# Pack attention and two MLPs on one core: the first MLP's output projection in thirds over two batches, the packs' products moved between its row tiles

## The chip, the cores and the metric

The kernel runs on 1 core of one Trainium2 chip. The metric is the device time of one execution in microseconds (us). The kernel before takes 1770.42 us, the median of 3 runs (1769.96 to 1776.33).

## What is computed

The reference has three stages in float32. Eight batches of 576 tokens and 8 heads go through a two-step attention over 32 pack tokens a head; its output, 4608 tokens of 512 features, goes through a gated MLP and then through a second MLP:

```python
p_packed = sm_attn(p, k, v)
out = sm_attn(q, p_packed, p_packed)
...
xn = x / rms * rms_g
g = xn @ w_gate
silu = g * (1.0 / (1.0 + np.exp(-g)))
val = xn @ w_val
return (silu * val @ w_out)
...
h = x @ w_in
g = h * (1.0 / (1.0 + np.exp(-1.702 * h)))
return (g @ w_out)
```

d_model is 512, d_ff is 1536 in the first MLP and 2048 in the second.

## The kernel before, in words

Every product of two float32 matrices is made of three matmuls, since each operand is split into a high and a low part (`h` and `l` in the tiles' names): high by high, high by low, low by high.

**Units, steps, pairs.** The first MLP takes the batches two at a time: a unit u holds batches 2u and 2u+1, called o = 0 and o = 1 in the code, so there are 4 units. A unit has 12 steps, one for each 128 of the 1536 features, and two steps (G = 2) make a pair. There are 48 steps and 24 pairs.

**A step** has two parts. `prods(s)` (L606) multiplies the packs (tiles Lh, Ll) with this step's gate and value weights: 12 matmuls of 256 columns into two PSUM tiles `ps_w` (L624), each copied out by two ACT casts (Wh, L626) and two DVE subtractions (Wl, L627). `gateval(s, o)` (L642) multiplies Wh, Wl with a batch's attention weights, in halves of 288 tokens: four groups of 6 matmuls into `ps_g` (L655). Of each half ACT takes a tanh (L662) and DVE two products (L663, L665); then ACT casts the 576 tokens to Hh (L670) and GpSimd subtracts for Hl (L671).

**The projection.** After two steps `close` (L713) runs `project` (L675) for o = 0, then o = 1, and in each for the 4 row tiles m of the output, in halves of 288 tokens: 16 groups of 6 matmuls of 288 columns into `ps_o` (L686), 96 in a pair. In a unit's first pair ACT copies a group to the accumulator (L693). Later m = 1, and m = 3 outside unit 0, are added by DVE from PSUM (L696); the others are copied by ACT (L700) and both halves added by one GpSimd instruction (L702). At a unit's end the accumulators go to DRAM (L706).

**Around it.** `ps_w`, `ps_g` and `ps_o` share 5 PSUM banks. The products of step s+1 run inside the o = 0 gate of step s: half of them after its first group, half after its last (L726 to L732). The weights `wg` (3 buffers) and `wo` (2 buffers) are loaded through SP's queue (L599, L604) in units 1 to 3; in unit 0 they are converted piece by piece on ACT, DVE and GpSimd (L98). Every generator yields a number of nanoseconds, and the loop at L985 spends them: attention work of the next unit runs in between in units 0 to 2. In unit 3 there is none left; there `early` (L822) converts weights of the second MLP, one weight for every 9 yields.

The kernel's text isn't the order on the engines: the framework plans each engine's order ahead of time (`schedule_with_timeline_sim=True`, L1058), with the order in the text as priority, and an instruction whose operands the plan sees ready may pass an earlier one whose operands it doesn't. On the chip each engine then keeps that order and waits where an operand comes later than planned.

The second MLP (L850, L869) has 3456 matmuls of 512 columns and isn't touched.

Of the kernel before, what the change touches and what calls it, by code (L numbers as in the profile page):

```python
# [9 lines left out]
F32 = mybir.dt.float32  # L10
F32R = mybir.dt.float32r
# [17 lines left out]
def tile_pack_attention__then__two_mlps(  # L29
# [14 lines left out]
    nc = tc.nc  # L44
    B, H, S, D = q.shape
# [7 lines left out]
    NT = B * S  # L53
    P = 128
    HS = S // 2
    NC = -(-S // P)
    REST = S - (NC - 1) * P
    GROUPS = (range(NC // 2), range(NC // 2, NC))
# [8 lines left out]
    G = 2  # L67
# [457 lines left out]
    def mlp1(cv, lp, mm, getL, getAT):  # L525
# [116 lines left out]
        def gateval(s, o):  # L642
            u, j = steps[s]
            Wh, Wl = Wp[s]
            Ah, Al = Aq[u, o]
            th = main.tile([P, S], F32, tag="th", name="th", bufs=3)
            for e in range(2):
                cols = slice(e * HS, (e + 1) * HS)
                pst = []
                for c in range(2):  # L650
                    ps = mm.tile([P, 512], F32, tag="mm", name="ps_g")[:, :HS]
                    n = 0
                    for g in range(NG):
# [12 lines left out]
                    if (e, c) != (1, 1):  # L666
                        yield 730
            Hh = main.tile([P, S], F32R, tag="Hh", name="Hh", bufs=2 * G)
            Hl = main.tile([P, S], F32R, tag="Hl", name="Hl", bufs=2 * G)
            nc.scalar.copy(Hh, th)  # L670
            nc.gpsimd.tensor_sub(Hl, th, fl(Hh))  # L671
            hh[s, o] = Hh, Hl
            yield 730

        def project(ss, o, m):  # L675
            u, j0 = steps[ss[0]]
            b = 2 * u + o
            for e in range(2):
                cols = slice(e * HS, (e + 1) * HS)
                ps = mm.tile([P, 512], F32, tag="mm", name="ps_o")[:, :HS]  # L680
                n = 0
                for s in ss:
                    oh, ol = wo[s][:, 0], wo[s][:, 1]
                    Hh, Hl = hh[s, o]
                    for st, mv in ((oh, Hh), (oh, Hl), (ol, Hh)):
                        nc.tensor.matmul(  # L686
                            ps, st[:, m * P : (m + 1) * P], mv[:, cols], start=n == 0, stop=n == 3 * len(ss) - 1
                        )
                        n += 1
                if j0 == 0:  # L690
                    if e == 0:
                        acc[o, m] = main.tile([P, S], F32, tag=f"acc{o}{m}", name=f"acc{o}{m}", bufs=1)
                    nc.scalar.copy(acc[o, m][:, cols], ps)  # L693
                elif m == 1 or m % 2 and u:
                    a = acc[o, m][:, cols]
                    nc.vector.tensor_add(a, a, ps)  # L696
                else:
                    if e == 0:
                        t = main.tile([P, S], F32, tag="add", name="add", bufs=2)
                    nc.scalar.copy(t[:, cols], ps)  # L700
                    if e == 1:
                        nc.gpsimd.tensor_add(acc[o, m], acc[o, m], t)  # L702
                if e == 0:
                    yield 365 * G
            if j0 + len(ss) == NF1:
                nc.sync.dma_start(x2_d[b][:, m], acc[o, m])  # L706
            yield 365 * G

        def run():
            nonlocal main  # L710
            main = pools["main"]

            def close(ss):  # L713
                for s in ss:
                    have(wo, s)
                for o in range(2):
                    for m in range(NM):
                        yield from project(ss, o, m)
                for t in ss:
                    Wp.pop(t)  # L720
                    wo.pop(t)
                    used["wo"] = t + 1
                    for o in range(2):
                        hh.pop((t, o))
# [12 lines left out]
            yield from both(0, 0, prods(1))  # L737
            yield from both(1, 0)
            yield "attention"
            scaled(0, 1)  # L740
            yield "next"
            yield from both(0, 1)
            yield from both(1, 1, prods(2))
            yield from close([0, 1])
            for s, (u, j) in enumerate(steps):
                if s < G:
                    continue
                load_wo(s)
# [12 lines left out]
        return fetch, piece, run  # L761
# [2 lines left out]
    def mlp2(pre, banks):  # L764
# [57 lines left out]
        def early():  # L822
            load_w(0)
            load_w(1)
            for _ in range(10):
                yield
            for n in range(4):
                split_w(n, keep(n, pre))
                for _ in range(9):
                    yield  # L830
            for f in range(2, 2 + NEARLY):
                t = pre.tile([P, NM, TT], F32R, tag=f"x{'hl'[f % 2]}", name="w2_stage", bufs=1)
                t = t.rearrange("p (i x) f -> p i x f", i=2)
                for x in range(2):
                    split_w(2 * f + x, t[:, x])
                    for _ in range(9):
                        yield
                nc.sync.dma_start(w2_d[f], fl(t))
                yield
# [76 lines left out]
    with ExitStack():  # L916
# [8 lines left out]
        with ExitStack() as st1:  # L925
# [59 lines left out]
            for what in run():  # L985
# [18 lines left out]
                else:  # L1004
# [7 lines left out]
                    while done >= PIECE:  # L1012
                        done -= PIECE
                        piece()
        with ExitStack() as st3:
            pools["pa"] = st3.enter_context(tc.tile_pool(name="pa", bufs=1, space=PSUM))
            pools["pm"] = st3.enter_context(tc.tile_pool(name="pm", bufs=4, space=PSUM))
# [45 lines left out]
```

## Time and profile before

| what | value |
|---|---|
| median of 3 runs | 1770.42 us |
| the profiled execution | 1774.51 us |
| its span, first to last instruction | 1772.7 us |
| mean granted TensorE clock, as a share of full speed | 0.99 |
| PE busy | 1713.1 us (97%) |
| PE's share of the chain that ended last | 80% |

The first units lie at about 80 to 340 us (unit 0), 340 to 567 (unit 1), 567 to 784 (unit 2) and 784 to 971 (unit 3); the second MLP follows. A matmul's duration in the trace includes the time in which its columns pass through the array while the next one has begun, so busy sums are larger than the time taken: the start-to-start distance is what one matmul takes from the engine.

### The profile page before, as it was taken

The numbers are of one execution on the slowest core, as the hardware profiler recorded it, in microseconds if no ns is written. First come the engines' busy times: TensorE is split into PE (matmuls) and PEld (weight loads), VectorE is DVE, ScalarE is ACT, GpSimd is POOL, SyncE is SP. The second block draws the span as 40 slices with busy tenths as digits, with TensorE's granted clock in tenths as the row PEclk, the third lists the DMA queues.
The fourth block names the chain that finished last, engine by engine and source line by source line (L and its number), as shares of the span: only waits on it lengthen the run. The fifth ranks groups of instructions, "written<-read, shape, count | busy, mean of one in ns | idle before, by whom it ended". The sixth has DMA issues, their size and how long they took to land.

```text
span 1772.7 us, 26286 instructions
## 1 busy us (share of the span) xinstructions
PE 1713.1 (97%) x9976; PEld 1513.4 (85%) x9976; DVE 912.2 (51%) x1971; ACT 699.5 (39%) x1644; POOL 495.8 (28%) x470
## 2 busy tenths in 40 slices
PE   7899989999999999999998999999999999999998
PEld 4579889999999999999988788888888888888887
DVE  5688898746756566667875662222222222222221
ACT  4567666655545655556553321111111111111111
POOL 2355666734553455434453220000000000000000
PEclk9899999999999999999999999999999999999999
DMA  9655565543334432255644620000000000000000
GB/s 228 163 161 148 184 190 191 179 154 121 126 115 164 138 122 85 96 196 201 236 170 161 249 84 24 25 24 24 24 25 24 24 24 24 24 1 24 2 23 24
DMA packets 154463, 186.27 MB, mean 105 GB/s; under 512 B 87648, under 2 KB 124512, under 8 KB 147296
## 3 DMA queue, kind: packets, MB, share of 16 engines
q1 hardware_dynamic: 154336, 184.58, 32.3%
q8 instruction: 79, 1.29, 0.3%
q14 instruction: 48, 0.39, 0.1%
HBM read 139.46 MB, written 45.09 MB: 104 GB/s over the span
## 4 chain that ended last, share of the span: by engine, by line
PE 80%; DVE 9%; DMA 5%; ACT 3%; issue 2%; SPq 1%; POOL 0%; DVEq 0%; ACTq 0%; POOLq 0%
PE ps_dn L876 22%; PE ps_up L857 22%; PE ps_o L686 14%; PE ps_g L655 11%; PE ps_at L266 2%; PE ps_w L624 2%; DVE Wl L627 2%; PE ps_at L311 2%; PE ps_at L388 2%; PE ps_at L255 1%; DMA raw<-in_moe_w_in_dram 1%; DVE th L663 1%; DMA raw<-in_moe_w_gate_dram 1%; DVE between L110 1%; DMA raw<-in_moe_w_val_dram 1%
## 5 line engine op out<-in xcount | busy, mean ns | idle before, releaser
L857 PE MATMUL ps_up<-xh,wi 128*128 128x512 f32 x1152 | 381.6, 393 | 2.3 <-DMA wi<-w 1.7
L876 PE MATMUL ps_dn<-wo,gh 128*128 128x512 f32 x1152 | 356.7, 391 | 0.0
L686 PE MATMUL ps_o<-Hh,wo 128*128 128x288 f32 x1536 | 330.9, 301 | 14.9 <-ACT add L700 4.9
L860 ACT ACTIVATE gf<-ps_up 128x512 f32<-128x512 f32 x144 | 85.9, 597 | 611.0 <-PE ps_up L857 590.2
L863 DVE CAST gh<-gf 128x512 fp32r<-128x512 f32 x144 | 62.3, 433 | 508.1 <-ACT gf L860 508.0
L686 PEld LDWEIGHTS ps_o<-Hh,wo 128*128 128x128 f32 x1536 | 254.6, 190 | 21.2 <-ACT add L700 6.2
L857 PEld LDWEIGHTS ps_up<-xh,wi 128*128 128x128 f32 x1152 | 216.2, 188 | 52.1 <-POOL wo L113 2.0
L876 PEld LDWEIGHTS ps_dn<-wo,gh 128*128 128x128 f32 x1152 | 216.2, 188 | 47.5
L655 PE MATMUL ps_g<-Aqh,Wh 128*128 128x288 f32 x768 | 235.6, 307 | 9.0 <-DVE th L663 4.4
L686 PE MATMUL ps_o<-Hl,wo 128*128 128x288 f32 x768 | 228.0, 298 | 0.0
L655 PE MATMUL ps_g<-Aqh,Wl 128*128 128x288 f32 x768 | 227.2, 297 | 0.0
L655 PE MATMUL ps_g<-Aql,Wh 128*128 128x288 f32 x768 | 226.7, 295 | 0.0
L857 PE MATMUL ps_up<-xl,wi 128*128 128x512 f32 x576 | 225.8, 392 | 0.0
L876 PE MATMUL ps_dn<-wo,gl 128*128 128x512 f32 x576 | 224.6, 391 | 0.0
L671 POOL TENSOR_TENSOR Hl<-th,Hh 128x576 fp32r<-128x576 f32 x96 | 137.6, 1433 | 207.6 <-ACT Hh L670 183.4
L655 PEld LDWEIGHTS ps_g<-Aqh,Wh 128*128 128x128 f32 x768 | 144.9, 189 | 16.6 <-DVE th L663 6.8
L702 POOL TENSOR_TENSOR acc<-acc,add 128x576 f32<-128x576 f32 x90 | 129.9, 1444 | 69.1 <-ACT add L700 68.5
L686 PEld LDWEIGHTS ps_o<-Hl,wo 128*128 128x128 f32 x768 | 146.1, 190 | 0.1
L655 PEld LDWEIGHTS ps_g<-Aqh,Wl 128*128 128x128 f32 x768 | 144.6, 188 | 1.0 <-DVE Wl L627 0.7
L655 PEld LDWEIGHTS ps_g<-Aql,Wh 128*128 128x128 f32 x768 | 145.0, 189 | 0.0
L627 DVE TENSOR_TENSOR Wl<-ps_w,Wh 64x512 fp32r<-64x512 f32 x192 | 131.7, 686 | 25.6 <-ACT Wh L626 22.2
L626 ACT CAST Wh<-ps_w 64x512 fp32r<-64x512 f32 x192 | 111.4, 580 | 46.4 <-PE ps_w L624 30.3
(150 smaller groups left out, 2591.3 us busy)
## 6 DMA issues: line engine op xcount, KB each, us to landing
wg<-wg SPq DMA_DIRECT2D x48, 1024.0 KB, 5.0
wo<-wo SPq DMA_DIRECT2D x48, 512.0 KB, 4.1
x<-acc SPq DMA_DIRECT2D x32, 288.0 KB, 2.4
out_dram<-ob SPq DMA_DIRECT2D x36, 256.0 KB, 2.0
vn<-in_v_dram SPq DMA_DIRECT2D x16, 512.0 KB, 5.4
qn<-in_q_dram SPq DMA_DIRECT2D x64, 128.0 KB, 3.6
raw<-in_moe_w_in_dram SPq DMA_DIRECT2D x16, 512.0 KB, 3.8
raw<-in_moe_w_out_dram SPq DMA_DIRECT2D x16, 512.0 KB, 3.5
```

Source lines behind the costliest of these rows:

```text
L266: nc.tensor.matmul(ps, x[:, a], y[:, a, span(e)], start=n == 0, stop=n == len(todo) - 1)
L311: nc.tensor.matmul(o, x[: size(c), c], v_of(y, c), start=i == 0, stop=i == len(todo) - 1,)
L626: nc.scalar.copy(Wh[rows, :, g], src)
L627: nc.vector.tensor_sub(Wl[rows, :, g], src, fl(Wh[rows, :, g]))
L655: nc.tensor.matmul(ps, st[:, o, g, c * P : (c + 1) * P], mv[:, g, cols], start=n == 0, stop=n == 3 * NG - 1)
L671: nc.gpsimd.tensor_sub(Hl, th, fl(Hh))
L686: nc.tensor.matmul(ps, st[:, m * P : (m + 1) * P], mv[:, cols], start=n == 0, stop=n == 3 * len(ss) - 1)
L702: nc.gpsimd.tensor_add(acc[o, m], acc[o, m], t)
L857: nc.tensor.matmul(ps, st[:, i], mv[:, i], start=n == 0, stop=n == 3 * NM - 1)
L860: nc.scalar.activation(gf, ps, AF.Gelu_apprx_sigmoid)
L863: nc.vector.tensor_copy(gh, gf)
L876: nc.tensor.matmul(pacc[r], st[:, r * P : (r + 1) * P], mv, start=f == 0 and n == 0, stop=f == NF2 - 1 and n == 2,)
```

## The change

The two batches of a unit lie behind each other in one tile (Hh, Hl and the accumulators have 1152 columns in place of 576), and `project` goes through them in thirds of 384 tokens: 4 row tiles by 3 thirds, 12 groups of 6 matmuls, 72 in a pair. The second third holds tokens of both batches. A third is added by a GpSimd instruction of its own. The products of the next two steps stand between the row tiles of `close`: one of their four groups behind each. `load_wo` of both steps stands at the pair's start, and `load_wg` behind both gates of a step. The nanoseconds yielded change with it (3 by 486 for 2 by 365 a batch), and `early` waits 8 yields for 9.

```diff
+    TS = 2 * S // 3
...
-            Hh = main.tile([P, S], F32R, tag="Hh", name="Hh", bufs=2 * G)
-            Hl = main.tile([P, S], F32R, tag="Hl", name="Hl", bufs=2 * G)
+            if o == 0:
+                hh[s] = [main.tile([P, 2, S], F32R, tag=f"H{x}", name=f"H{x}", bufs=G) for x in "hl"]
+            Hh, Hl = (t[:, o] for t in hh[s])
             nc.scalar.copy(Hh, th)
             nc.gpsimd.tensor_sub(Hl, th, fl(Hh))
...
-        def project(ss, o, m):
+        def project(ss, m):
+
             u, j0 = steps[ss[0]]
-            b = 2 * u + o
-            for e in range(2):
-                cols = slice(e * HS, (e + 1) * HS)
-                ps = mm.tile([P, 512], F32, tag="mm", name="ps_o")[:, :HS]
+            for e in range(3):
+                cols = slice(e * TS, (e + 1) * TS)
+                ps = mm.tile([P, 512], F32, tag="mm", name="ps_o")[:, :TS]
...
-                    if e == 0:
-                        t = main.tile([P, S], F32, tag="add", name="add", bufs=2)
-                    nc.scalar.copy(t[:, cols], ps)
-                    if e == 1:
-                        nc.gpsimd.tensor_add(acc[o, m], acc[o, m], t)
-                if e == 0:
-                    yield 365 * G
+                    t = main.tile([P, TS], F32, tag="add", name="add", bufs=3)
+                    nc.scalar.copy(t, ps)
+                    a = acc[m][:, cols]
+                    nc.gpsimd.tensor_add(a, a, t)
+                if e < 2:
+                    yield 486 * G
             if j0 + len(ss) == NF1:
-                nc.sync.dma_start(x2_d[b][:, m], acc[o, m])
-            yield 365 * G
+                for o in range(2):
+                    nc.sync.dma_start(x2_d[2 * u + o][:, m], acc[m][:, o * S : (o + 1) * S])
+            yield 486 * G
...
-            def close(ss):
+            def close(ss, ahead=()):
...
-                for o in range(2):
-                    for m in range(NM):
-                        yield from project(ss, o, m)
+                rest = (ns for s in ahead for ns in prods(s))
+                for m in range(NM):
+                    yield from project(ss, m)
+                    yield next(rest, 0)
+                yield from rest
...
-            yield from both(1, 1, prods(2))
-            yield from close([0, 1])
-            for s, (u, j) in enumerate(steps):
-                if s < G:
-                    continue
-                load_wo(s)
-                yield from both(s, 0, prods(s + 1))
-                load_wg(s + WGB)
-                yield from both(s, 1)
-                if j == NF1 - 1:
+            yield from both(1, 1)
+            Wp.clear()
+            yield from close([0, 1], [2, 3])
+            for s in range(G, len(steps), G):
+                u, j = steps[s]
+                ss = list(range(s, s + G))
+                for t in ss:
+                    load_wo(t)
+                for t in ss:
+                    for o in range(2):
+                        yield from both(t, o)
+                    Wp.pop(t)
+                    load_wg(t + WGB)
+                last = j + G == NF1
+                if last:
                     yield "attention"
                     scaled(u + 1, 0)
                     scaled(u + 1, 1)
-                if j % G == G - 1:
-                    yield from close(list(range(s - G + 1, s + 1)))
-                if j == NF1 - 1:
+                yield from close(ss, [t + G for t in ss])
+                if last:
                     yield "unit"
...
-            for _ in range(10):
+            for _ in range(6):
                 yield
...
-                for _ in range(9):
+                for _ in range(8):
                     yield
```

## Rows read from the trace of the kernel before

**Rows 1.** The page: busy time of the engines, and the granted clock in slices.

```profile
PE 1713.1 (97%) x9976; PEld 1513.4 (85%) x9976; DVE 912.2 (51%) x1971; ACT 699.5 (39%) x1644; POOL 495.8 (28%) x470
...
PEclk9899999999999999999999999999999999999999
```

**Rows 2.** Busy time by stretch: unit 0, unit 3, second MLP (stretch, length, busy).

```profile
80.00:340.00 260.00, 240.66 (x1677) 222.32 (x1677) 223.22 (x576) 178.80 (x483) 159.09 (x168) 0.97 0.55 170
...
784.00:971.00 187.00, 176.60 (x1286) 170.81 (x1284) 139.86 (x265) 103.30 (x212) 86.65 (x63) 0.99 0.55 193
971.00:1772.70 801.70, 794.83 (x3456) 648.35 (x3456) 225.53 (x387) 129.27 (x221) 20.24 (x15) 1.00 0.11 38
```

**Rows 3.** The same view for most of units 1 and 2.

```profile
350.00:750.00 400.00, 400.00 (x3016) 390.71 (x3015) 246.03 (x550) 223.15 (x546) 182.56 (x162) 1.00 0.39 124
```

**Rows 4.** Waits of PE in unit 3: total us, times, longest us.

```profile
PE ps_g L655 <- DVE Wl L627: 3.3, 3, 2.6
PE ps_g L655 <- DVE th L663: 2.1, 3, 0.9
PE ps_w L624 <- DVE th L665: 1.0, 1, 1.0
```

**Rows 5.** Timeline of PE: a projection's first matmul, and the next pair's first gate matmul.

```profile
891.72 0.29 PE L686 MATMUL ps_o<-Hh,wo 128*128 128x288 f32 x1
...
904.47 0.29 PE L655 MATMUL ps_g<-Aqh,Wh 128*128 128x288 f32 x1
```

**Rows 6.** Groups by line and shape: instructions that are cut anew or moved.

```profile
L686 PE MATMUL ps_o<-Hh,wo 128*128 128x288 f32 x1536 | 330.9, 301 | 14.9 <-ACT add L700 4.9 <-DVE th L663 4.3 <-ACT acc L693 2.5
...
L671 POOL TENSOR_TENSOR Hl<-th,Hh 128x576 fp32r<-128x576 f32 x96 | 137.6, 1433 | 207.6 <-ACT Hh L670 183.4 <-issue 16.8 <-PE ps_w L624 3.1
L627 DVE TENSOR_TENSOR Wl<-ps_w,Wh 64x512 fp32r<-64x512 f32 x192 | 131.7, 686 | 25.6 <-ACT Wh L626 22.2
L702 POOL TENSOR_TENSOR acc<-acc,add 128x576 f32<-128x576 f32 x90 | 129.9, 1444 | 69.1 <-ACT add L700 68.5
L626 ACT CAST Wh<-ps_w 64x512 fp32r<-64x512 f32 x192 | 111.4, 580 | 46.4 <-PE ps_w L624 30.3 <-DVE Wl L627 13.7
...
L700 ACT COPY add<-ps_o 128x288 f32<-128x288 f32 x180 | 70.3, 400 | 95.4 <-PE ps_o L686 94.5
```

**Rows 7.** Timeline of PE in the second MLP: eight matmuls of 512 columns.

```profile
1299.62 0.39 PE L857 MATMUL ps_up<-xl,wi 128*128 128x512 f32 x1
...
1301.44 0.62 PE L876 MATMUL ps_dn<-wo,gh 128*128 128x512 f32 x2
```

**Rows 8.** Timeline of PE in unit 3: a wait, and 12 matmuls later.

```profile
947.55 0.58 PE L655 MATMUL ps_g<-Aqh,Wh 128*128 128x288 f32 x1 [2.61 <-DVE Wl L627]
...
950.57 0.31 PE L655 MATMUL ps_g<-Aqh,Wh 128*128 128x288 f32 x1
```

**Rows 9.** Sums over unit 3's six gate stretches (first group to projection).

```profile
sum 106.29, PE 98.42 PEld 94.12 DVE 90.94 ACT 67.12 POOL 39.90; mean PE 16.40 PEld 15.69 DVE 15.16 ACT 11.19 POOL 6.65
```

**Rows 10.** Sums over unit 3's six projections.

```profile
sum 80.68, PE 78.15 PEld 76.66 DVE 48.92 ACT 36.17 POOL 46.72; mean PE 13.03 PEld 12.78 DVE 8.15 ACT 6.03 POOL 7.79
```

**Rows 11.** Timelines of PE, DVE, ACT and POOL: last gate group to Hl, unit 3.

```profile
859.58 0.29 PE L655 MATMUL ps_g<-Aqh,Wl 128*128 128x288 f32 x1
...
862.25 0.45 DVE L665 SCALAR_TENSOR_TENSOR th<-th,ps_g 128x288 f32<-128x288 f32 x1
...
862.73 0.68 ACT L670 CAST Hh<-th 128x576 fp32r<-128x576 f32 x1 [0.83 <-DVE th L665]
...
861.98 1.44 POOL L702 TENSOR_TENSOR acc<-acc,add 128x576 f32<-128x576 f32 x1 [2.38 <-ACT add L700]
863.49 1.43 POOL L671 TENSOR_TENSOR Hl<-th,Hh 128x576 fp32r<-128x576 f32 x1
```

**Rows 12.** The page, DMA issues: KB each, median us to landing.

```profile
wg<-wg SPq DMA_DIRECT2D x48, 1024.0 KB, 5.0
wo<-wo SPq DMA_DIRECT2D x48, 512.0 KB, 4.1
```

More of the change, by code (lines that the diff above doesn't have):

```diff
@@ L667, in gateval @@
                         yield 730
-            Hh = main.tile([P, S], F32R, tag="Hh", name="Hh", bufs=2 * G)
-            Hl = main.tile([P, S], F32R, tag="Hl", name="Hl", bufs=2 * G)
+            if o == 0:
+                hh[s] = [main.tile([P, 2, S], F32R, tag=f"H{x}", name=f"H{x}", bufs=G) for x in "hl"]
+            Hh, Hl = (t[:, o] for t in hh[s])
             nc.scalar.copy(Hh, th)
             nc.gpsimd.tensor_sub(Hl, th, fl(Hh))
-            hh[s, o] = Hh, Hl
             yield 730
-        def project(ss, o, m):
+        def project(ss, m):
             u, j0 = steps[ss[0]]
-            b = 2 * u + o
-            for e in range(2):
-                cols = slice(e * HS, (e + 1) * HS)
-                ps = mm.tile([P, 512], F32, tag="mm", name="ps_o")[:, :HS]
+            for e in range(3):
+                cols = slice(e * TS, (e + 1) * TS)
+                ps = mm.tile([P, 512], F32, tag="mm", name="ps_o")[:, :TS]
                 n = 0
@@ L683, in project @@
                     oh, ol = wo[s][:, 0], wo[s][:, 1]
-                    Hh, Hl = hh[s, o]
+                    Hh, Hl = (t.rearrange("p o t -> p (o t)") for t in hh[s])
                     for st, mv in ((oh, Hh), (oh, Hl), (ol, Hh)):
@@ L691, in project @@
                     if e == 0:
-                        acc[o, m] = main.tile([P, S], F32, tag=f"acc{o}{m}", name=f"acc{o}{m}", bufs=1)
-                    nc.scalar.copy(acc[o, m][:, cols], ps)
+                        acc[m] = main.tile([P, 2 * S], F32, tag=f"acc{m}", name=f"acc{m}", bufs=1)
+                    nc.scalar.copy(acc[m][:, cols], ps)
                 elif m == 1 or m % 2 and u:
-                    a = acc[o, m][:, cols]
+                    a = acc[m][:, cols]
                     nc.vector.tensor_add(a, a, ps)
                 else:
-                    if e == 0:
-                        t = main.tile([P, S], F32, tag="add", name="add", bufs=2)
-                    nc.scalar.copy(t[:, cols], ps)
-                    if e == 1:
-                        nc.gpsimd.tensor_add(acc[o, m], acc[o, m], t)
-                if e == 0:
-                    yield 365 * G
+                    t = main.tile([P, TS], F32, tag="add", name="add", bufs=3)
+                    nc.scalar.copy(t, ps)
+                    a = acc[m][:, cols]
+                    nc.gpsimd.tensor_add(a, a, t)
+                if e < 2:
+                    yield 486 * G
             if j0 + len(ss) == NF1:
-                nc.sync.dma_start(x2_d[b][:, m], acc[o, m])
-            yield 365 * G
+                for o in range(2):
+                    nc.sync.dma_start(x2_d[2 * u + o][:, m], acc[m][:, o * S : (o + 1) * S])
+            yield 486 * G
         def run():
@@ L711, in run @@
             main = pools["main"]
-            def close(ss):
+            def close(ss, ahead=()):
                 for s in ss:
                     have(wo, s)
-                for o in range(2):
-                    for m in range(NM):
-                        yield from project(ss, o, m)
+                rest = (ns for s in ahead for ns in prods(s))
[3 more added lines that the diff above has]
+                yield from rest
                 for t in ss:
-                    Wp.pop(t)
                     wo.pop(t)
+                    hh.pop(t)
                     used["wo"] = t + 1
-                    for o in range(2):
-                        hh.pop((t, o))
             def both(s, o, ahead=None):
@@ L835, in early @@
                     split_w(2 * f + x, t[:, x])
-                    for _ in range(9):
+                    for _ in range(8):
                         yield
@@ L1014, in tile_pack_attention__then__two_mlps @@
                         piece()
+            for _ in ahead:
+                pass
         with ExitStack() as st3:
```

## The prediction

> **What bounds the kernel now.** I read the page first: PE is busy for 97% of the span and the granted clock is near full in all slices [rows 1], so only fewer PE nanoseconds or fewer PE waits can change the time. Busy time by stretch then tells where PE idles. The second MLP, 801.7 us of the span, isn't touched. Over 400 us of units 1 and 2 PE has no idle time at all [rows 3]. Unit 0 leaves 260.0 - 240.7 = 19.3 us idle and unit 3 187.0 - 176.6 = 10.4 us [rows 2]. So the steady state is bound by the rate at which PE takes columns, and the two outer units lose some to waits. Third, the waits in unit 3: PE waits 3.3 us for Wl, the packs' products on their way out through DVE, and 2.1 and 1.0 us for the gate's products in `th` [rows 4]. Last, the timeline, for the distance from one matmul to the next: a projection's 96 matmuls take 904.47 - 891.72 = 12.75 us [rows 5], 132.8 ns each, while the mean duration on the page is 301 [rows 6].
>
> **Part A: 72 matmuls of 384 columns for 96 of 288.** The columns are the same, so what goes is whatever each matmul costs beside its columns. No row has 384 columns. The nearest are 288 at 132.8 ns and 512, eight of which take 301.44 - 299.62 = 1.82 us [rows 7], 227.5 ns each. The line through both gives 132.8 + 96 x 94.7/224 = 173.4 ns for 384. 72 x 173.4 = 12.48 us for 12.75: 0.27 us a pair, **6.4 us** over 24 pairs. The whole second MLP is slower, 801.7/3456 = 232.0 ns [rows 2]; the line to that gives 175.3 ns and 3.1 us saved, which is one bound. The other end is the rows' rounding: if the eight took 1.81 us, the line gives 172.8 ns and 7.4 us. I take 6.4, from matmuls in a row at full clock like the projection's.
> The fixed part can be held against a rule. The Trainium skill, "TensorE: Matmul & The Clock Gate", section "Back-to-back issue gap", gives N/2.4 + 2.5 ns for the distance at full clock. By that 576 matmuls would save 1.4 us; here the trace disagrees with 132.8 ns, where the rule gives 122.5.
>
> **Part B: the products leave the gate.** In a pair 24 matmuls, 8 ACT casts of 580 ns and 8 DVE subtractions of 686 ns [rows 6] move from the gate into the projection. PE's own work is the same. What it frees is in unit 3, where weight conversions share DVE: there DVE is busy 90.9 of 106.3 us in the gate stretches [rows 9] and 48.9 of 80.7 in the projections [rows 10]. Taking 8 x 0.686 = 5.5 us a pair out leaves DVE (90.9 - 32.9)/6 = 9.7 us in a gate that takes 12.8 us of PE; the projection goes to (48.9 + 32.9)/6 = 13.6 us in about 15.3. Then: the waits for Wl go, 3.3 us, since each product now has at least two row tiles or a whole gate of the first step ahead of its use. With the 2.61 us wait goes what it did to the clock: the 12 matmuls behind it took 950.57 - 947.55 = 3.02 us [rows 8] where 12 x 0.1328 = 1.59, nearly twice as long each, as at the lower of the clock's two levels: 1.4 us. Of the 3.1 us for `th` I take half, 1.5 (bounds 0 and 3.1). What is late next is the projection itself, whose PSUM banks wait for DVE and ACT: 0.5 us back (bounds 0 and 3). **B = 5.7 us**, bounds 1.7 and 7.8. Outside unit 3 I take nothing from B: units 1 and 2 have no idle time to give.
>
> **Part C: the projection needs o = 1 sooner.** Before, a projection began with o = 0 and came to o = 1 after 48 matmuls, 6.4 us. Now its second third holds tokens of o = 1. In the text's order 6 matmuls of the first third, 3 of the first step and one with Hh come before the first that reads the late Hl: 10 x 0.173 = 1.7 us. In unit 3 Hl came later than that: the last gate matmul starts at 859.58, DVE ends `th` at 862.70, ACT Hh at 863.41, and GpSimd, which does an addition first, Hl at 864.92 [rows 11]: 5.2 us after the projection's first matmul at 859.71. So 3.5 us are uncovered if PE keeps the text's order. But the plan knows DVE, ACT and GpSimd's queues too (that the addition is ahead of Hl shows that it expected Hh no earlier), and it has work to pull forward: the first thirds of three more row tiles, 18 x 0.173 = 3.1 us, and the packs' products, 24 x 0.119 = 2.9 us by the line of part A at 256 columns. Cover is 6.0 us, if PSUM banks are free. What remains is the time by which the chip is later than the plan. In units 1 and 2, full of attention work tied together as closely, this leaves no idle time [rows 3]: 0 there. In units 0 and 3 ACT and DVE wait for converted weights, which the plan can't know; I take 0.35 us a pair for 12 pairs, **4 us** lost (bounds 0 and 24 x 3.5 = 84, if no work is pulled forward).
>
> **Part D: edits without a price.** ACT's copies and GpSimd's additions are cut anew: ACT 3 copies of 400 to 533 ns (as is, or by columns) for 4 of 400, GpSimd 3 additions of 963 to 1444 ns for 2 of 1444 [rows 6]. GpSimd may grow by 45 x 1.444 = 65 us at worst, but it is 28% busy [rows 1]; in unit 3's projections it is busy 7.8 of 13.4 us [rows 10], and if that cover is gone the additions delay Hl, which is part C. `load_wo` of both steps waits at the pair's start for the last projection's end; behind it on SP's queue stand weights for conversion and `wg`. The load lands in 4.1 us, `wg` in 5.0 [rows 12], and the projection is a gate of 12.8 us away, so nobody waits; `load_wg` no longer waits for products, which by then lie a projection back. The stores at a unit's end go out two by two, with the second MLP's reads much later. `early` has 8 of 192 yields a weight for 9 of 216: the same pace. Hh's buffer is freed at the projection's end for both batches; its next writer comes after four gate groups, 3.2 us. Unit 0 gets another order of conversions, with ACT's projection fuller: between 5 us better and 10 worse, taken as 0, since its total work is the same.
>
> **Sum.** -6.4 - 5.7 + 4 = -8.1 us. The profiled execution took 1774.51 us (span 1772.7 and 1.8 around it), so one like it would take 1766.4. The median of the runs is 4.1 us below that execution; I give the time on the median's scale: **1762.3**, or 1762.
>
> **Rivals.** *The columns cost what they cost* (0.15): spacing is proportional, 384 take 177.1 ns and A is nothing; 1768.7. For it: the second MLP's mean of 232.0 ns is near proportional (236.1). Against: eight of its matmuls in a row at 227.5. The rule of the Trainium skill named above would put it between, at 1767.3. *The projection waits for Hl* (0.14): slower. The place is the second third of the first row tile in each pair; price 3.5 us a pair if nothing is pulled forward, and with half of it covered 24 x 1.75 = 42 us, in place of the 4 taken: 1800. It decides from (8.85 + 12.1)/24 = 0.87 us a pair on. For it: Hl comes 5.2 us late in the row, with an addition ahead of it. Against: units 1 and 2 without idle time. *More waits go* (0.16): unit 0 also profits, 5 us of its 19.3, C costs nothing and `th` no longer waits: -6.4 - 7.3 - 5 = -18.7; 1752. The forecast itself has 0.55, between 1756 and 1768.
>
> **The numbers.** About 0.5% (8.85 us) is what a measurement of this kernel can tell from no change; the bounds are 1761.6 and 1779.3. The forecast lies next to the lower one: of its 0.55 I give 0.23 to faster and 0.32 to same; the third rival adds 0.16 to faster, the first 0.15 to same, and of the second 0.13 is slower and 0.01 same. Faster 0.39, same 0.48, slower 0.13. The range leaves out the dear end of the Hl wait and the best end of the third rival: 1750 to 1778.
>
> **What would show it.** A: L686's count is 1728 and a projection's 72 matmuls without a gap take 12.5 us plus the products' 2.8. B: no wait on Wl is left in unit 3, its gate stretches shrink from 17.7 us towards 13, DVE's busy time in them to about 10. C: PE's waits at L686 for Hl or Hh sum to some 4 us, all in units 0 and 3. I am wrong if units 1 and 2 show idle time at the second third, if unit 0 grows by over 10 us, or if 384 columns are spaced at 177 ns.

## The result, and the profile after

The changed kernel takes 1740.1 us, the median of 4 runs (1738.92 to 1741.57), against 1770.19 us before: a ratio of 0.9819, 95% interval 0.9803 to 0.9836. It is 30 us faster, where 8 were forecast, and below the range of the forecast. The profiled execution took 1741.26 us with a span of 1739.5.

The page of the changed kernel, busy times and clock, beside [rows 1]:

```profile
PE 1698.6 (98%) x9400; PEld 1501.6 (86%) x9400; DVE 908.5 (52%) x1936; ACT 690.1 (40%) x1583; POOL 502.3 (29%) x515
...
PEclk9899999999999999999999999999999999999999
```

To see where 33.3 us of span went (the profiled execution before lies 4.3 us above its median, the one after 1.2 us), I cut both traces at the first gate matmul of each unit and at the second MLP's first matmul. Busy time by stretch, the kernel before: units 0 to 3, second MLP (stretch, length, then busy time of PE and PEld, TensorE's matmuls and weight loads, DVE, which is VectorE, ACT, which is ScalarE, and POOL, which is GpSimd):

```profile
90.77:357.42 266.65, 248.60 (x1761) 232.59 (x1761) 223.48 (x575) 180.01 (x479) 169.92 (x175) 0.98 0.56 177
357.42:567.20 209.78, 209.78 (x1582) 204.84 (x1581) 129.17 (x287) 117.23 (x288) 94.69 (x83) 1.00 0.40 130
567.20:784.03 216.83, 213.99 (x1617) 209.23 (x1616) 137.55 (x302) 122.69 (x296) 96.92 (x87) 1.00 0.39 128
784.03:971.30 187.27, 176.57 (x1286) 170.81 (x1285) 140.01 (x265) 103.30 (x212) 86.67 (x63) 0.99 0.55 193
971.30:1772.74 801.44, 794.83 (x3456) 648.32 (x3456) 225.38 (x386) 129.27 (x221) 20.18 (x14) 1.00 0.11 38
```

The same stretches of the changed kernel:

```profile
88.16:341.61 253.45, 245.84 (x1652) 231.42 (x1652) 226.24 (x576) 183.16 (x478) 172.81 (x191) 0.99 0.60 187
341.61:551.43 209.82, 209.82 (x1441) 203.52 (x1439) 129.98 (x280) 113.88 (x267) 98.07 (x95) 1.00 0.42 132
551.43:760.69 209.26, 209.26 (x1450) 204.66 (x1448) 133.17 (x287) 116.78 (x274) 95.72 (x94) 1.00 0.38 128
760.69:938.50 177.81, 170.07 (x1130) 165.40 (x1129) 137.26 (x253) 99.33 (x196) 87.70 (x72) 1.00 0.58 205
938.50:1739.46 800.96, 794.85 (x3456) 648.38 (x3456) 225.49 (x386) 129.57 (x221) 20.50 (x14) 1.00 0.11 38
```

Unit 0 is 13.2 us shorter, units 1 and 2 together 7.5, unit 3 9.5, the second MLP 0.5. The stretch ahead of the first gate is 2.6 us shorter, but in the experiments' traces it lies between 84.0 and 91.0 us for kernels whose text is the changed kernel's up to there, so I count it for nothing.

Columns: a projection of unit 3 without a wait, in the timeline of PE:

```profile
833.41 0.33 PE L687 MATMUL ps_o<-Hh,wo 128*128 128x384 f32 x1
...
848.06 0.40 PE L625 MATMUL ps_w<-wg,Lh 128*128 128x256 f32 x2
...
848.77 0.29 PE L656 MATMUL ps_g<-Aqh,Wh 128*128 128x288 f32 x1
```

The last of four product groups takes 0.71 us; 15.36 - 4 x 0.71 = 12.52 us for 72 matmuls, 173.9 ns each. Before it was 12.75 for 96 [rows 5]: 0.23 a pair, 5.5 us over 24.

What the prediction never looked at is unit 0 by its stages. Sums over its six gate stretches and its six projections, the kernel before, then after:

```profile
sum 156.39, PE 145.92 PEld 135.06 DVE 147.80 ACT 112.54 POOL 83.89; mean PE 24.32 PEld 22.51 DVE 24.63 ACT 18.76 POOL 13.98
sum 110.26, PE 102.68 PEld 97.53 DVE 75.68 ACT 67.47 POOL 86.03; mean PE 17.11 PEld 16.26 DVE 12.61 ACT 11.25 POOL 14.34
```

```profile
sum 117.01, PE 115.02 PEld 109.02 DVE 114.14 ACT 82.41 POOL 65.83; mean PE 19.17 PEld 18.17 DVE 19.02 ACT 13.73 POOL 10.97
sum 136.44, PE 130.82 PEld 122.41 DVE 112.10 ACT 100.75 POOL 106.97; mean PE 21.80 PEld 20.40 DVE 18.68 ACT 16.79 POOL 17.83
```

Before, DVE was busy 147.80 of 156.39 us in unit 0's gates, 95%, and 69% in its projections. PE was idle for 156.39 - 145.92 = 10.5 us in the gates and 7.6 in the projections; after it is 2.0 and 5.6.

The granted clock has a part in it too. Three of unit 0's six projections before and one after hold a piece at 0.50, the lower of the clock's two levels (stretch, length, busy times, then the mean granted clock):

```profile
118.86:140.40 21.54, 19.01 (x127) 18.00 (x127) 13.66 (x34) 14.73 (x37) 12.65 (x16) 0.92 0.69 210
167.71:188.40 20.69, 18.68 (x127) 17.74 (x126) 16.96 (x46) 13.58 (x37) 17.98 (x20) 0.92 0.53 168
262.08:279.91 17.83, 16.30 (x109) 15.84 (x109) 13.15 (x36) 9.83 (x29) 14.10 (x14) 0.90 0.56 177
```

```profile
197.06:224.18 27.12, 24.97 (x149) 23.32 (x148) 24.26 (x64) 17.22 (x44) 22.07 (x28) 0.94 0.57 182
```

Each piece begins about where a wait of PE ends, of 1.2 to 2.5 us, for a copy by ACT. Length times what the clock lacks to 1.00 gives 5.2 us lost before and 1.6 after, so some 3.5 of unit 0's 13.2 us are clock that came back with the waits.

### The profile page after: what moved, and what is told of

Its sections match the earlier page's. It is cut to its first block, busy times and chain, and to the rows that moved or that the text cites. A ratio compares the mean times of both kernels' runs of the same rounds, so it can differ in the third digit from the quotient of the medians.

```text
span 1739.5 us, 25121 instructions
## 1 busy us (share of the span) xinstructions
PE 1698.6 (98%) x9400; PEld 1501.6 (86%) x9400; DVE 908.5 (52%) x1936; ACT 690.1 (40%) x1583; POOL 502.3 (29%) x515
## 4 chain that ended last, share of the span: by engine, by line
PE 86%; DVE 5%; DMA 4%; ACT 2%; issue 1%; POOL 1%; DVEq 0%; ACTq 0%; SPq 0%; POOLq 0%
PE ps_dn L882 23%; PE ps_up L863 23%; PE ps_o L687 14%; PE ps_g L656 14%; PE ps_w L625 3%; PE ps_at L267 3%; PE ps_at L256 2%; PE ps_at L312 2%; PE ps_at L389 2%; DVE Wl L628 1%; DMA raw<-in_moe_w_in_dram 1%; DMA raw<-in_moe_w_out_dram 1%; DMA raw<-in_moe_w_gate_dram 1%; DMA kw<-in_k_dram 1%; DVE w L112 1%
## 5 line engine op out<-in xcount | busy, mean ns | idle before, releaser
L687 PE MATMUL ps_o<-Hh,wo 128*128 128x384 f32 x1152 | 325.2, 341 | 5.2 <-ACT add L700 3.5
L687 PEld LDWEIGHTS ps_o<-Hh,wo 128*128 128x128 f32 x1152 | 210.5, 189 | 11.4 <-ACT add L700 4.8
L687 PE MATMUL ps_o<-Hl,wo 128*128 128x384 f32 x576 | 194.5, 338 | 0.6 <-POOL Hl L673 0.6
L702 POOL TENSOR_TENSOR acc<-acc,add 128x384 f32<-128x384 f32 x135 | 136.5, 1023 | 58.7 <-ACT add L700 57.5
L882 PEld LDWEIGHTS ps_dn<-wo,gl 128*128 128x128 f32 x576 | 108.1, 188 | 24.7
```

Source lines behind the costliest of these rows:

```text
L687: nc.tensor.matmul(ps, st[:, m * P : (m + 1) * P], mv[:, cols], start=n == 0, stop=n == 3 * len(ss) - 1)
L702: nc.gpsimd.tensor_add(a, a, t)
L882: nc.tensor.matmul(pacc[r], st[:, r * P : (r + 1) * P], mv, start=f == 0 and n == 0, stop=f == NF2 - 1 and n == 2,)
```

## The experiments

All medians are of 4 to 10 runs, beside 4 to 22 runs of the kernel before made with them; "unit 0" and "units 1 to 3" are lengths between first gate matmuls in the profiled execution, as above.

| run | median us | ratio to before (95%) | unit 0 | units 1 to 3 |
|---|---|---|---|---|
| before | 1770.19 | | 266.7 | 613.9 |
| after | 1740.10 | 0.9819 (0.9803 to 0.9836) | 253.4 | 596.9 |
| e1_thirds | 1757.07 | 0.9909 (0.9891 to 0.9926) | 259.8 | 606.0 |
| e2_products | 1750.56 | 0.9873 (0.9854 to 0.9892) | 263.4 | 598.4 |
| e3_rowwise | 1749.26 | 0.9866 (0.9843 to 0.9889) | 261.0 | 599.0 |
| e4_loads | 1772.85 | 1.0005 (0.9988 to 1.0021) | 268.8 | 615.4 |
| e5_rows | 1761.37 | 0.9943 (0.9926 to 0.9960) | 267.5 | 608.9 |
| c1_before_364 | 1776.10 | 1.0014 (0.9996 to 1.0032) | 265.9 | 617.0 |
| c2_before_367 | 1772.10 | 0.9996 (0.9978 to 1.0014) | 268.3 | 615.4 |
| c3_thirds_485 | 1755.85 | 0.9910 (0.9877 to 0.9942) | 257.8 | 605.2 |
| c4_after_485 | 1743.74 | 0.9836 (0.9797 to 0.9875) | 255.8 | 597.9 |
| d1_unit0 | 1780.03 | 1.0028 (1.0005 to 1.0051) | 292.6 | 598.4 |
| d2_units12 | 1747.00 | 0.9854 (0.9813 to 0.9895) | 252.1 | 604.5 |
| d3_unit0_rows | 1755.72 | 0.9913 (0.9879 to 0.9948) | 266.8 | 596.7 |
| e6_pieces | 1757.89 | 0.9918 (0.9895 to 0.9941) | 270.2 | 600.7 |
| f1_rows_6banks | 1754.43 | 0.9898 (0.9876 to 0.9920) | 265.1 | 607.9 |
| f2_thirds_4banks | 1786.10 | 1.0078 (1.0058 to 1.0098) | 280.9 | 597.0 |
| f3_after_6banks | 1749.49 | 0.9872 (0.9849 to 0.9894) | 256.8 | 611.0 |
| f4_rows_4banks | 1783.96 | 1.0076 (1.0049 to 1.0103) | 281.2 | 599.4 |
| g1_unit3_8banks | 1730.50 | 0.9777 (0.9741 to 0.9813) | 250.5 | 586.8 |

**The parts by themselves.** e1: the changed `project`, with the products and loads as before (cut from its edit of the changed kernel).

```diff
                 for m in range(NM):
                     yield from project(ss, m)
-                    yield next(rest, 0)
...
+                yield from both(s, 0, prods(s + 1))
```

> The projection in thirds over both batches alone; the products of the next step and the loads stay where the kernel before has them. Theory 1 (unit 0's gates are bound by VectorE, and the moved products' subtractions, 33 us of VectorE work over its six pairs, are what freed them): only the columns' 6 us go, 1764 us, unit 0 about as long as before (266 us from the first gate group to unit 1's). Theory 2 (the thirds: fewer and longer groups, fewer copies out, fewer bank waits): 1745 to 1750, unit 0 near 253 us. Theory 3 (another order of loads and conversions): 1764.

e2: the kernel before with the products and loads moved, `project` untouched (cut from its edit of the kernel before).

```diff
                 for o in range(2):
                     for m in range(NM):
                         yield from project(ss, o, m)
+                        if m % 2:
+                            yield next(rest, 0)
```

> The products moved between the row tiles alone (one of four groups behind every second row tile), with the loads in the changed kernel's order; the projection keeps halves of 288, batch by batch. Theory 1: 1740 + 6 = 1746 us, unit 0 near 255 us, with VectorE's share in its gates still over 0.95 and their length down by some 35 us, the projections' up by about 20. Theory 2: 1764 to 1770. Theory 3: 1746 too, told apart by the run with the loads alone.

e3: as e2, with the loops over m and o changed about and the products behind each m.

> As the run with the products alone, but each row tile takes o = 0 and then o = 1 (halves of 288), so o = 1 is needed after 12 matmuls as in the changed kernel. If the earlier need of Hl costs what the prediction took (4 us), 4 us over the run with the products alone, 1750; if the plan covers it, the same within 2 us.

e4: the loads alone. e5: the loops over m and o changed about in the kernel before, nothing else.

```diff
-                load_wo(s)
+                if j % G == 0:
+                    load_wo(s)
+                    load_wo(s + 1)
                 yield from both(s, 0, prods(s + 1))
-                load_wg(s + WGB)
                 yield from both(s, 1)
+                load_wg(s + WGB)
```

> The loads' order alone: both wo at the pair's start, wg behind both gates of a step; all else as before. Theories 1 and 2: 1770 within 3 us. Theory 3: 1750 to 1755 or so, with the gain in unit 0 or at the units' ends.

> The order of the projection alone: row tile by row tile, o = 0 then o = 1 in each, halves of 288; the products and loads as before. Against the run with the thirds alone (1757, 16 us under the kernel before) only the width of a group differs. If the order gives what the thirds gave beyond their columns, 1762; if the width does (a group of 384 holds its PSUM bank for 1.04 us of matmuls in place of 0.80, so that a late copy has longer before the banks run out, and there are 9 late copies where there were 12), 1772 within 3 us, and unit 0 stays near 266 us with its waits of ps_o for ACT.

The loads alone do nothing. Both other parts gain, and in unit 0 they gain in different stages. Gate stretches, then projections, of e1:

```profile
sum 153.34, PE 144.12 PEld 133.10 DVE 146.50 ACT 114.11 POOL 87.78; mean PE 24.02 PEld 22.18 DVE 24.42 ACT 19.02 POOL 14.63
sum 106.48, PE 103.11 PEld 97.39 DVE 77.74 ACT 67.09 POOL 84.37; mean PE 17.19 PEld 16.23 DVE 12.96 ACT 11.18 POOL 14.06
```

And of e2:

```profile
sum 119.09, PE 115.81 PEld 109.59 DVE 110.31 ACT 82.51 POOL 67.96; mean PE 19.30 PEld 18.27 DVE 18.39 ACT 13.75 POOL 11.33
sum 144.30, PE 132.96 PEld 126.62 DVE 114.53 ACT 102.72 POOL 102.30; mean PE 22.16 PEld 21.10 DVE 19.09 ACT 17.12 POOL 17.05
```

PE's idle time in the gates is 10.5 us before, 9.2 with the thirds alone, 3.3 with the products moved. In the projections it is 7.6 before, 3.4 with the thirds, 11.3 with the products moved: what they load onto the projections they partly give back there. Together: 2.0 and 5.6. Theory 1 expected 1764 of e1 and an unchanged unit 0, and was wrong in that; the thirds help unit 0's projections by themselves. It was wrong on e2 too, where it expected unit 0 near 255: e2's gates are 37 us shorter, as it had it, but its projections 34 us longer where it had 20, and unit 0 is at 263.4, 3.3 us shorter and no more. e5 shows that it is the thirds and not the order: unit 0 stays at 267.5. e5's median does come out at 1761.4, what was expected if the order gave the gain, but not in unit 0: in its trace the lead is 83.54 us for 90.77, though the text is the same up to there (the granted clock is at 0.50 for 6.8 us of it, for 20.5 before, which is 6.8 of these 7.2 us), and units 1 to 3 are 5 us shorter, 3 of them a stall at the end of unit 2 that the kernel before has. So the readings below go by the stages' lengths and not by the medians alone. e3 and e2 differ by 1.3 us, within their spread: the earlier need of o = 1 costs nothing that shows.

**The plan by itself.** Since any edit changes the planned order, the four c runs change a number only: `yield 365 * G` to 364 and 367 in the kernel before, `yield 486 * G` to 485 in e1 and in the changed kernel.

> How far the plan alone moves the time: the kernel before, with a projection's group counted as 364 x 2 ns in place of 365 x 2. Nothing is computed otherwise, attention work and conversions only fall a little later between the groups. If the gains seen so far are effects of the parts, the median stays within 4 us of 1772 and unit 0 within 3 us of 266.7; if they are accidents of the plan, both move by 7 us or more.

> The same with 367 x 2 ns, so that they fall a little earlier: within 4 us of 1772 and unit 0 within 3 us of 266.7, or else an accident of the plan is as large as the effects.

> The run with the thirds alone, a group counted as 485 x 2 ns for 486 x 2. If the thirds' 7 us in unit 0 beyond their columns are an effect of the width, unit 0 stays at 260 within 3 us and the median at 1757 within 4; if they were an accident, unit 0 goes back towards 266.

> The changed kernel, a group counted as 485 x 2 ns for 486 x 2: 1740 within 4 us, unit 0 at 253 within 3 us, if the whole gain isn't an accident of its plan.

Unit 0 stays within 2.4 us of its kernel in all four, the medians within 6 us (c1's is 4.1 us from 1772, where 4 were allowed). With e4 and e5 the kernel before's unit 0 has five traces between 265.9 and 268.8; the thirds' two and the changed kernel's two stand clear of them. The products' 263.4 lies 2.5 us below the lowest, about as much as a change of the plan alone can do: of e2 only the shift between the stages is clear, not its 3.3 us in unit 0.

**A dose of VectorE work.** d1 and d2 put two VectorE instructions behind each gate of unit 0, or of units 1 and 2; d3 two behind each row tile of unit 0. Their result isn't read.

```diff
             nc.gpsimd.tensor_sub(Hl, th, fl(Hh))
+            if u == 0:
+                extra = main.tile([P, S], F32, tag="extra", name="extra", bufs=1)
+                nc.vector.tensor_scalar(extra, th, LEAST_WORD, None, op0=ALU.max)
+                nc.vector.tensor_scalar(extra, th, LEAST_WORD, None, op0=ALU.max)
```

> The changed kernel with two more VectorE instructions behind each gate of unit 0 (128x576, their result isn't used), 48 in all at some 0.4 to 0.75 us, 19 to 36 us of VectorE work. Theory 1 (VectorE binds unit 0's gates): the kernel gets slower by half of that work or more, 10 us at least. Rival (VectorE's share is high but PE waits for other things, ACT and its DMA above all): under 4 us.

> The same addition in units 1 and 2 only, 96 instructions, twice the work of the other run. Theory 1: nothing there is bound by VectorE, so under 5 us in all. Rival (any VectorE work in the gates delays the chain that PE needs): 20 us or more.

> The changed kernel with the same 48 extra VectorE instructions in unit 0 as the run with them behind the gates (44.7 us of work there, 40 us slower), two behind each of the 24 row tiles of its projections, where VectorE is busy 82% of the time and not 98%. If it is the place that counts (gates bound by VectorE, projections not), half the loss or less: 1750 to 1760. If VectorE's total binds unit 0, as much as there: 1775 or more.

Busy time by stretch: unit 0 of d1, units 1 and 2 of d2, unit 0 of d3 (DVE is the third busy time).

```profile
87.36:379.94 292.58, 258.94 (x1661) 233.83 (x1661) 263.08 (x626) 184.09 (x479) 176.53 (x191) 0.99 0.52 162
```

```profile
343.12:561.18 218.06, 215.75 (x1476) 209.54 (x1475) 165.46 (x344) 117.44 (x275) 107.42 (x103) 0.99 0.42 133
561.18:770.16 208.98, 206.07 (x1412) 201.46 (x1411) 153.84 (x319) 112.66 (x267) 93.32 (x85) 0.99 0.37 124
```

```profile
84.20:351.02 266.82, 253.08 (x1659) 231.20 (x1658) 250.07 (x623) 183.02 (x480) 178.75 (x190) 1.00 0.58 179
```

Behind unit 0's gates 263.08 - 226.24 = 36.8 us more of DVE's busy time make the unit 292.58 - 253.45 = 39.1 us longer. Behind its row tiles 23.8 us make it 13.4 longer. In units 1 and 2 56.2 us (319.30 for 263.15) make them 8.0 longer, of which 3.4 are 6.8 us at the clock's lower level that the changed kernel doesn't have there. In the medians d1 is 40 us slower than the changed kernel, as theory 1 had it, d3 15.6, inside its 1750 to 1760, and d2 6.9, between its two theories' bounds.

The added instructions don't all run where the text puts them. Unit 0's gate stretches, then projections, of d1, and of d3:

```profile
sum 143.13, PE 124.83 PEld 112.87 DVE 138.32 ACT 84.89 POOL 73.35; mean PE 20.80 PEld 18.81 DVE 23.05 ACT 14.15 POOL 12.23
sum 149.45, PE 134.12 PEld 120.96 DVE 124.76 ACT 99.21 POOL 103.18; mean PE 22.35 PEld 20.16 DVE 20.79 ACT 16.53 POOL 17.20
```

```profile
sum 126.98, PE 122.65 PEld 111.90 DVE 122.95 ACT 85.35 POOL 76.35; mean PE 20.44 PEld 18.65 DVE 20.49 ACT 14.23 POOL 12.72
sum 139.84, PE 130.42 PEld 119.30 DVE 127.12 ACT 97.67 POOL 102.40; mean PE 21.74 PEld 19.88 DVE 21.19 ACT 16.28 POOL 17.07
```

In d1 29 of the 48 start in gates and 19 in the first 9 us of a projection. DVE's busy time grows by 24.2 us in the gates, which get 26.1 us longer, and by 12.7 in the projections, which get 13.0 longer. In d3 12 start in gates and 36 more than 8 us into a projection: 8.8 us more in the gates make them 10.0 longer, 15.0 in the projections 3.4. So a microsecond of DVE's time costs 1.1 us in unit 0's gates in both runs, about 1 at the start of its projections, 0.23 later in them, and 0.14 in units 1 and 2.

This shows that DVE binds unit 0's gates. It doesn't give the size of the gain. Before, 45 of the subtractions in unit 0 (30.8 us) started in its gates, after it still 14 (9.6 us), so 21 us left the gates and not the 33 of the expectation; at 1.1 us there and 0.23 later they would have bought some 18 us, where e2 gives 3.3 in unit 0, and the changed kernel 6.4 beyond e1. The prices are also of the changed kernel only. And ACT's casts (6 pairs of 8 x 0.580 = 28 us) moved together with the subtractions: no run moves one without the other.

e6 tried to buy more of it, by moving unit 0's weight conversions towards the projections.

```diff
-                    done += what
+                    done += what * (0.6 if what == 730 else 1.33)
```

> The changed kernel, with unit 0's conversions of weights spread otherwise: a gate's nanoseconds count 0.6 and all others 1.33 towards the next conversion, so that of some 13.7 conversions a pair 3.7 lie at the gates and 10 at the projections, where VectorE is busy 82% of the time in place of 98%. Theory 1: unit 0 gets shorter, by 3 to 8 us, 1733 to 1737. Rival: within 3 us of the changed kernel, either side.

It got slower: 1757.9 us, unit 0 270.2. Its gate stretches and projections in unit 0:

```profile
sum 118.77, PE 114.26 PEld 108.58 DVE 101.52 ACT 77.03 POOL 61.77; mean PE 19.04 PEld 18.10 DVE 16.92 ACT 12.84 POOL 10.29
sum 151.46, PE 137.00 PEld 126.70 DVE 120.64 ACT 102.63 POOL 111.23; mean PE 22.83 PEld 21.12 DVE 20.11 ACT 17.10 POOL 18.54
```

DVE's share in the gates fell to 85%, but they didn't get shorter: in the changed kernel PE is already busy for 115.02 of their 117.01 us, so there was nothing to win there. The projections got 15.0 us longer. PE's idle time in them grew from 5.6 to 14.5 us, and the granted clock took 6.9 us more: it was at 0.94, 0.84 and 0.94 in three projections of 27.26, 32.32 and 27.98 us, 8.5 us lost for 1.6. 5.6 us of PE's waits in unit 0 are for a conversion's last step:

```profile
PE ps_at L389 <- ACT Ah L135: 5.8, 1, 5.8
PE ps_o L687 <- DVE w L112: 5.6, 5, 2.0
```

In the code a conversion's tile `between` lies in one of the first MLP's five PSUM banks (L107 of the changed kernel), beside `ps_w`, `ps_g` and `ps_o`; that step is its last reader. So conversions, too, take banks from the projections that they were moved to.

**PSUM banks.** Why does the width help? I supposed the five banks, and changed how the eight are shared between the first MLP and the attention (`MMB = 5` to 6 or 4, the rest for the attention); the waits at ps_o in the expectations are sums of the distances between matmul starts beyond their usual ones, where that is over 0.2 us.

> The run with the order by row tiles in halves (1761, unit 0 267.5 us, 10.6 us of waits over 0.2 us at ps_o there), with six PSUM banks for the first MLP and two for the attention in place of five and three. Bank theory: the waits at ps_o in unit 0 fall to 6 us or less and unit 0 to about 261, unless the attention's own waits grow by as much. Rival (the width helps by fewer instructions on ACT and VectorE): waits at ps_o within 2 us of 10.6.

> The run with the thirds alone (1757, unit 0 259.8, 5.4 us of waits at ps_o) with four banks and four for the attention. Bank theory: four banks of 1.04 us are about as good as five of 0.80, so waits at ps_o go back to 9 us or more. Rival: within 2 us of 5.4.

> The changed kernel with six banks and two for the attention. Bank theory: at ps_o, ps_g and ps_w in unit 0 there are 7.5 us of waits over 0.2 us to win, of which half, 1736; the attention with two banks may give it back. Rival: 1740 or slower.

> The order by row tiles in halves with four banks, four for the attention. Bank theory: waits at ps_o in unit 0 grow from 10.6 us to 15 or more, and unit 3, where VectorE is late too, gets longer by 3 us or more. Rival: both as with five banks within 2 us.

By the same sums, waits at ps_o in unit 0 fell from 10.6 to 5 us with six banks, as the bank theory had it, but those at ps_g rose from 6 to 10 and the attention's from 4 to 13, and unit 0 is only 2.4 us shorter. That length doesn't decide: f1's unit 0 holds 73 matmuls fewer than e5's, and 20.5 us of it are at the clock's lower level, for 6.8. With four banks the thirds' waits at ps_o are 6.6 us, as the rival had it, and the halves' 1.7, against both; in both runs those at ps_g doubled or more, to 16.2 and 13.3, and the kernels are slower than the one before. (f4's unit 3 was expected to grow by 3 us or more; it has 174 matmuls fewer than e5's and can't be compared.) Six banks in the changed kernel make units 1 to 3 14 us longer, and f3 comes out at 1749.5, on its rival's side. So banks are worth much, on either side, but that they are the reason for the thirds' gain in unit 0 isn't shown; it stays open.

In unit 3, where no attention competes, f1 is plain: 175.42 us for e5's 185.98 with the same matmuls. That led to a version: g1 is the changed kernel, with the attention's three banks given to the first MLP once the attention is over.

```diff
+            if "more" in pools and turns[0] % 8 > 4:
+                return pools["more"].tile(shape, F32, tag="more", name=name)
...
                         st2.close()
+                        pools["more"] = st1.enter_context(tc.tile_pool(name="more", bufs=3, space=PSUM, side="right"))
```

> The changed kernel with the attention's three PSUM banks given to the first MLP in unit 3, where there is no attention left: ps_w, ps_g and ps_o turn among eight. If banks held by late copies are what unit 3's remaining 12 us beyond its matmuls' distances come from, unit 3 goes from 178 to 172 us or less and the median to 1734 or less; if VectorE's own lateness is, 177 and 1739 to 1740.

1730.5 us, 0.9777 of the kernel before, for 0.9819: 7 to 10 us under the changed kernel, as the ratios or the medians are taken, though the ratios' intervals touch. The profiled execution (1723.03) is the fastest of its four, 7.5 us under the median, and part of what its lead and unit 0 show is that. Gates now run ahead of projections, so the cuts between units blur: units 1 to 3 take 586.8 us for 596.9. From the last unit's first gate matmul on, its stretch is

```profile
745.27:921.29 176.02, 175.17 (x1184) 174.03 (x1183) 140.42 (x261) 101.70 (x203) 93.63 (x77) 1.00 0.63 220
```

with 0.9 us of idle time for 7.7 before the edit. The expected 1734 or less came; unit 3's length can't be held against the expected 172, since the stretch has 54 matmuls more than before the edit.

## Why the prediction was wrong

**The step that failed is the price of unit 0**: "Unit 0 gets another order of conversions [...] between 5 us better and 10 worse, taken as 0", and in part B "Outside unit 3 I take nothing from B". With its share of A (1.6 us won) and of C (2 us lost) unit 0 was to stay as it was; it gave 13.2 us, although its stretch holds one step's products more (12 matmuls, 1.4 us) and 22 attention matmuls more than before. That is the larger part of the miss; units 1 and 2 gave 7.5 for 3.2, unit 3 9.5 for 5.3.

What was wrong in it is PE's waits: idle time in unit 0 fell from 18.1 to 7.6 us, and the clock lost to waits from 5.2 to 1.6. Two parts of the change took them, which the prediction priced at nothing there beyond the thirds' columns.

The products are one. The row that should have said so was there: DVE is busy for 223.22 of 260.00 us in unit 0 [rows 2], 86%, where unit 3, which part B treated as bound by DVE, has 75%. I split unit 3 by stage and not unit 0. Split, its gates show DVE at 95%, and part B's own reasoning applies with more force: e2 takes 7.2 us of PE's idle time from these gates (and puts 3.7 into the projections), and d1 and d3 show that DVE's time there costs its full length. The argument "since its total work is the same" was wrong: the same 48 instructions cost 39.1 us behind the gates and 13.4 behind the row tiles.

The thirds are the other, and by themselves the larger: e1 shortens unit 0 by 6.9 us, of which part A's columns are 1.4 (6 pairs of 0.23). They take PE's idle time in the projections from 7.6 to 3.4 us. That it isn't the order is shown (e5); why the thirds help is not, it stays open. The products alone give 3.3 us, and 3.0 of the 13.2 come only with both.

**Part A** held: 5.5 us for 6.4, spacing 173.9 ns for 173.4. The proportional rival (177 ns) is out. So is, for this stream, the rule that gave 1.4 us (162.5 ns by it, 173.9 measured): the Trainium skill, "TensorE: Matmul & The Clock Gate", section "Back-to-back issue gap", states it for an isolated matmul.

**Part B** held for unit 3 in its sum, less so in its terms. The wait for Wl fell from 3.3 to 0.3 us and the gate stretches from 106.3 to 82.2, 13.7 us each. DVE's busy time in a gate came down to 11.8 us only (70.8 over six), where 9.7 were predicted, because 20.1 us left the gates and not 32.9: 13 subtractions still run there. Waits of PE in unit 3 after, beside [rows 4]:

```profile
PE ps_g L656 <- DVE th L664: 2.5, 3, 1.7
...
PE ps_o L687 <- ACT add L700: 1.0, 2, 0.7
...
PE ps_o L687 <- ACT Hh L672: 0.6, 1, 0.6
PE ps_o L687 <- POOL Hl L673: 0.6, 1, 0.6
PE ps_g L656 <- DVE Wl L628: 0.3, 1, 0.3
```

Of the 9.5 us, 1.4 are products that now lie ahead of the unit's first gate and 1.4 are columns; the remaining 6.7, by difference, are waits and what they did to the clock, for 5.7 in B: PE's idle time fell by 3.0 us (10.7 to 7.7), 1.7 are the clock, which no longer falls behind the wait of [rows 8], and no row shows the other 2.0 one by one. Of the 1.5 us that I took for `th` 0.6 came (2.1 and 1.0 before, 2.5 now). Units 1 and 2 gave 7.5: 2.8 columns, 3.1 a stall at the end of unit 2 (the start distance of 3.13 us there is gone), the rest probably attention that runs in unit 0 now. The prediction missed that stall, since [rows 3] ends at 750 us and it lies at 768 to 771: these units did have 2.8 us of idle time to give.

**Part C**, the wait for Hl, was taken as 4 us, half of it in unit 0. It is 1.2, the two rows for Hh and Hl above, all in unit 3; unit 0 shows no such wait. The plan pulls other work forward, as the prediction said (in the projection at 833.41 the first products start 12 matmuls in, where the text has them after 18), and the rival that would have made the kernel slower has no support: e3 needs o = 1 early and isn't slower than e2.

**Part D**, otherwise: the loads are free (e4). No run tries ACT's and GpSimd's new sizes by themselves; what was taken as free with them is the thirds' gain in unit 0. The groups by line after, for [rows 6]: GpSimd's sum grew by 6.6 us, ACT's copies shrank by 7.2.

```profile
L702 POOL TENSOR_TENSOR acc<-acc,add 128x384 f32<-128x384 f32 x135 | 136.5, 1023 | 58.7 <-ACT add L700 57.5
...
L700 ACT COPY add<-ps_o 128x384 f32<-128x384 f32 x135 | 63.1, 481 | 39.9 <-PE ps_o L687 38.3 <-POOL Lh L343 0.5
```

The third rival, "more waits go", named unit 0 and gave it 5 us and a chance of 0.16; it was the nearest, but unit 0 gave 13.2, and `th` is still waited for.

## What to carry to other kernels

An engine's busy share is worth reading by stage before a stage is called unbound: unit 0's 86% for DVE was 95% in the gates and 69% in the projections, and PE's idle time in the gates fell by 7.2 us when work left them. What a microsecond of an engine's work costs at a place can be measured by adding some there (1.1 in the gates, 0.23 late in the projections, 0.14 in units 1 and 2 here), if the stages are read for where it really ran. That says which place is bound; here it did not say what a move gains, since part of what left one stage came back in the next. Where a stage left PSUM banks unused, giving them to the first MLP took 7 to 10 us more.

## What the runs showed of the hardware

The added VectorE instructions were expected to take 0.4 to 0.75 us each. With GpSimd idle they take about 0.45 us, but some take up to 2.36. Timeline of d1, VectorE, then GpSimd:

```profile
151.69 0.45 DVE L676 TENSOR_SCALAR extra<-th 128x576 f32<-128x576 f32 x1
...
152.75 1.08 DVE L677 TENSOR_SCALAR extra<-th 128x576 f32<-128x576 f32 x1
...
157.72 1.06 DVE L676 TENSOR_SCALAR extra<-th 128x576 f32<-128x576 f32 x1
```

```profile
152.08 1.44 POOL L673 TENSOR_TENSOR Hl<-th,Hh 128x576 fp32r<-128x576 f32 x1 [1.40 <-ACT Hh L672]
...
157.03 1.43 POOL L673 TENSOR_TENSOR Hl<-th,Hh 128x576 fp32r<-128x576 f32 x1 [2.62 <-ACT Hh L672]
```

The short one starts while GpSimd is idle. The long ones start while it is busy and end 0.31 and 0.32 us after its instruction does. Over d1, d2 and d3 all 70 that took more than 0.6 us started with a GpSimd instruction running, and 66 of them ended 0.31 to 0.33 us after it. Not every overlap does this: 7 others took 0.44 to 0.46 us although a GpSimd instruction had 0.5 us or more to go. The Trainium skill, "SBUF — State Buffer", section "Who interferes with whom", says that the two engines share a port pair, that some copies and tensor_scalar forms on VectorE take it, and that whoever comes second is blocked until the first is done. The trace agrees for the 66, with 0.32 us after the end. For d1 this means that a part of the 36.8 us is VectorE waiting for GpSimd: 48 instructions of 0.45 us would be 21.6 us. The prices above are of VectorE's busy time with that wait in it.
